# Another order of the same steps in a gated-recurrence and bilinear-FFN kernel

## The chip, the core and the metric

The kernel runs on one core of one Trainium2 chip. A core has five engines that run side by side, each from a queue of its own in the order in which the program issues: TensorE (PE in the profile, with its weight loads as PEld), VectorE (DVE), ScalarE (ACT), GpSimd (POOL) and SyncE (SP, which here only issues DMAs). The metric is device time in microseconds (us) of one execution, as the median of several runs.

## What is computed

The reference is a gated linear recurrence over time, followed by a bilinear feed-forward network on its output:

```python
for t in range(S):
    state = alpha[:, :, t, :, None] * state + np.einsum('bhd,bhe->bhde', k[:, :, t], v[:, :, t])
    y[:, :, t] = np.einsum('bhd,bhde->bhe', q[:, :, t], state)
x = y.transpose(0, 2, 1, 3).reshape(B * S, H * D)
out = (x @ w_a) * (x @ w_b) @ w_out
```

q, k, v and alpha are 4 batches x 8 heads x 768 steps x 48 in float32; w_a and w_b are 384 x 1536, w_out is 1536 x 384; the output is 3072 x 384 float32.

## The kernel before

**Chunks.** Time is cut into three stretches of 256 steps and the batches into two pairs, which makes six chunks (0 to 5). A chunk holds two batches (u = 0 and 1); each partition holds two neighbouring time steps (r), and the 128 partitions are two groups g of 64, that is, two blocks of 128 time steps. Even chunks belong to one pair of batches, odd chunks to the other, and a chunk takes over the state of the chunk two before it. Each chunk goes through a recurrence part and then a feed-forward part on its 512 tokens. PE works on the feed-forward part of one chunk while DVE, ACT and POOL prepare the recurrence of the next.

**The order** is written out by hand in a string, PROGRAM (lines 17 to 356 before). Each line names a chunk and then steps, and the kernel issues them in exactly that order: so every engine's queue is the order of its own steps in the string. A trailing letter gives the engine where there is a choice (V = DVE, S = ACT, P = POOL, Y = SP). Trailing digits on PE's steps are the PSUM banks (0 to 7) they write. A step that writes a bank or a buffer waits for its last reader.

The steps of the recurrence, with the line that does the work:

- `ld a|k|q|v` (L503) loads an input of the chunk; `W` (L483) and `Wo` (L486) load weights. SP or POOL issues them.
- `ln` (L510, ACT) takes the logarithm of alpha; `l2`, `l2s` (L518, L567) add it over the pair of time steps; `H`, `L` (L555, L561) and `R` (L577) split the sum into parts for PE; `B`, `A2`, `AQ` (L545, L592, L587) are the cumulative sums on PE.
- `E .. i|b` (L621, ACT) takes their exponentials; `ra` (L599, ACT) and `lv` (L606) adjust k and q for the second step of the pair; `mk`, `mq` (L632, DVE) scale k and q by them into QKp.
- `dk`, `de` (L654, L675) or, in later chunks, `dr`, `dl` (L638, L643: two small DMAs by way of DRAM) bring the decay of a group.
- `C`, `Ce` (L692; L914 or L916) transpose QKp on PE and copy the result out of PSUM; chunks 2 to 5 use `T` (L701, a DMA transpose issued by SP) and `Tr` (L914 or L916) in their place.
- `v`, `vs` (L725 or L727; L914 or L916) copy v into vx, straight and with the two halves of a group crossed. `vs` is two copies of 32 partitions for each u.
- `K`, `K2` (L748, L761) are the state's products, `k` (L775, or L778 and L779, DVE) updates the state; `D` (L793) are the scores; `M` (L802, DVE) masks them out of PSUM, or `Mc` (L806, ACT) copies them and `Mm` (L810, DVE) masks in SBUF.
- `SB`, `SA` (the carried state) and `Y` (inner products; all L822) add up y in PSUM, two banks for each u; `X` (L858 on ACT, L860 on DVE) copies it to xT.

The feed-forward steps: `a f w`, `b f w` (L877) are the up-projections of 128 of the 1536 columns (f = 0 to 11): three matmuls of 512 tokens (w = *), or of 256 (w = 0 or 1, one u only, which can start after that u's X). `as` (L883, ACT) copies a's bank to one of three SBUF buffers, `pr` (L891, DVE) multiplies it by b's bank. `o m h` (L899) is half of the down-projection of 128 tokens, six matmuls; `oc` (L910) the same for half the columns, at the very end; `ot`, `otc` (L914 or L916) copy the result and `st`, `stc` (L932, L935) store it.

Every matmul of the recurrence's products, scores and y is done in 64-row, 64-column pieces, four side by side; the feed-forward ones take the whole 128 x 128 array. Going from one shape to the other and back happens some 60 times in PE's order.

The loads of chunks 0 to 2, those of v for all, and all weights are on POOL's queue (chunk 0's first loads excepted); the other loads of chunks 3 to 5, the DMA transposes, the decay's DMAs and the stores are on SP's.

Of the kernel before, what the change touches and what calls it, by code (L numbers as in the profile page):

```python
# [18 lines left out]
0: B 0a 0; ld q 0b Y; E 0b i; mk 0b V; dk 0 4; E 0b b; mq 0b V; C 0 1 5; E 0a i; mk 0a V; E 0a b; fill 2 0; ld v 0 P; ld q 0a Y; mq 0a V; de 0; Ce 0 1 V; ld a 1 P  # L19
0: ln 1; cs 0 m P; C 0 0 1; Ce 0 0 V; ld k 1 P; K 0 0 2; k 0 0 V; ld q 1 P; cm 1; D 0 1 4; M 0 1; D 0 0 0; M 0 0; v 0 S; vs 0 1 V; SB 0 2; vs 0 0 V; B 1a 6  # L20
0: E 1a b; mq 1a V; E 1a i; mk 1a V; B 1b 4; W b 0 256; E 1b b; mq 1b V; dk 1 0; E 1b i; de 1; C 1 0 1; cz 0 v P; Y 0; SA 0; mk 1b V; C 1 1 0; Ce 1 0 V
0: Ce 1 1 V; D 1 0 4; ld v 1 P; K 1 0 1; K 1 1 6; X 0 S; v 1 S; Mc 1 0; D 1 1 2; Mc 1 1; W a 256 768; a 3 0 0; a 4 0 7; k 1 0 V; cz 1 q P; as 4 0; vs 1 0 V; a 5 0 1
0: W a 0 256; a 0 0 4; as 5 0; vs 1 1 V; Mm 1 0 V; SB 1 2; W b 256 768; b 4 0 5; Mm 1 1 V; cs 1 m P; b 3 0 1; a 1 0 7
1: ld a 0 P; ld a 1 P
0: k 1 1 V; a 2 0 6; as 2 0; pr 4 0; K 0 1 5; k 0 1 V; SA 1; Y 1; b 2 0 6; pr 2 0; b 1 0 5; as 1 0; pr 1 0; b 5 0 7; pr 5 0; W a 768 1536; X 1 S; c2 P
0: b 2 1 2; a 2 1 3; W b 768 1536; a 1 1 5
1: ld q 0 P
0: b 0 0 6
1: ln 0; l2 0 V; ld k 0 P
0: a 0 1 7  # L30
1: ld v 0 P
0: as 0 0; pr 0 0
1: ld q 1 P
0: as 3 0; a 5 1 0; b 0 1 4; as 2 1; pr 3 0; as 0 1; a 10 * 3; a 6 * 1
1: H 0 V; L 0 V
0: a 7 * 6; b 4 1 7; pr 2 1; a 4 1 2; pr 0 1; Wo 0 6; b 6 * 4
1: ln 1; l2 1 V; H 1 V
0: as 6 *; pr 6 *; b 10 * 1; as 10 *; a 8 * 3
1: ra 0; lv 0 q P; ld k 1 P; A2 0 4
0: as 4 1; pr 4 1; pr 10 *; a 9 * 2; a 3 1 1; Wo 6 12  # L40
1: L 1 V
2: ld a * P
1: ld v 1 P; E 0 b
0: b 8 * 7
1: E 0 i
0: as 3 1; as 9 *
2: ld q * P
1: lv 0 k V; mk 0 V
0: b 3 1 1; pr 3 1
1: dk * 4; de *  # L50
0: b 9 * 1
1: A2 1 2; mq 0 V
0: pr 9 *; as 7 *; as 8 *; as 5 1
1: E 1 b
0: b 7 * 4; pr 7 *
1: E 1 i
0: a 11 * 6; as 1 1
1: C 0 0 0; C 0 1 1
0: b 11 * 2; b 1 1 3
1: ra 1; lv 1 q P  # L60
0: pr 8 *; as 11 *; pr 11 *; b 5 1 4; pr 5 1
1: lv 1 k P
0: o 2 0 5
1: Ce 0 0 S; D 0 0 6; v 0 S; K2 0 0 0 2
0: pr 1 1; o 1 0 3; o 3 0 4
1: Mc 0 0; mq 1 V; Ce 0 1 S; D 0 1 6; k 0 0 V; SB 0 0; Mm 0 0 V; k 0 1 V; vs 0 0 S
0: o 3 1 -; ot 3 S
1: mk 1 V; C 1 0 2
2: ln *
1: vs 0 1 V; M 0 1  # L70
0: o 1 1 -
1: Ce 1 0 V
0: ot 1 S
1: v 1 V
2: l2s 0 V; l2 0 V
1: C 1 1 4; Ce 1 1 S
0: o 2 1 -
1: K2 1 1 2 3
2: ld k * P; l2s 1 V; ra 0
1: vs 1 0 S  # L80
3: ld v * P
0: cz 1 v P
1: Y 0; k 1 0 V; SA 0
0: st 3 Y
1: X 0 S; vs 1 1 V; D 1 1 6; Mc 1 1
2: R 0
1: k 1 1 V
0: o 0 0 4; o 0 1 -; c3 P
3: ld a * P
1: a 2 0 0  # L90
# [12 lines left out]
1: pr 1 0
2: AQ 6; E 1 b; E 1 i; E 0 i
1: b 10 0 1; pr 10 0; b 4 0 2; pr 4 0
2: mk 1 V; E 0 b
1: a 7 0 5; as 7 0
2: lv 1 q P
1: Y 1; SA 1; X 1 S; a 0 0 1; a 6 0 2; as 6 0
2: mq 0 V  # L110
1: b 7 0 5; pr 7 0; b 8 0 6
2: mq 1 V
1: b 5 0 7; b 6 0 2; a 3 0 3; a 10 1 4; as 5 0; pr 5 0; a 11 0 0; b 3 0 5; b 0 0 7; pr 6 0; b 10 1 2
3: ln *
2: dr
1: as 3 0; pr 3 0; a 6 1 3; as 0 0
2: T 1
1: pr 0 0; b 11 0 1; a 8 0 5
3: ra 1
1: as 11 0; pr 11 0; a 2 1 7; as 10 1; pr 10 1; b 2 1 4; a 1 1 0  # L120
2: dl
1: b 6 1 1; as 8 0; as 2 1; pr 8 0; a 0 1 2
3: l2 0 P
1: a 5 1 5; pr 2 1; a 9 0 4; b 9 0 6; b 5 1 7; as 6 1; pr 6 1
2: lv 0 k P; mk 0 V; T 0
3: v 0 S
1: as 9 0; pr 9 0; a 3 1 1; b 3 1 3; as 5 1; pr 5 1
2: K2 * * 4 5
3: vs 0 0 V; ra 0
1: b 9 1 6; as 3 1  # L130
4: ld a * Y
1: pr 3 1; a 9 1 1; o 2 0 3; o 2 1 -
2: k * 0 V; k * 1 V
3: vs 0 1 S
0: st 1 Y
1: b 0 1 7
2: Tr 1 V; v 0 S; vs 0 1 V
3: ld q * Y
1: b 7 1 4; as 0 1; pr 0 1; as 9 1; as 1 1
3: ld k * Y  # L140
1: b 8 1 2; a 7 1 5; ot 2 S
2: v 1 S; vs 1 1 P
3: l2s 0 P
1: as 7 1
4: ld k * Y
3: v 1 V
1: pr 9 1; b 1 1 3; pr 1 1; pr 7 1; a 11 1 0
2: Tr 0 S; D 1 1 6; M 1 1
1: a 4 1 1; as 4 1; a 8 1 3; o 0 0 4; as 11 1
3: l2s 1 P  # L150
1: as 8 1; pr 8 1
2: D 0 0 0; Mc 0 0; D 1 0 6; Mc 1 0
1: b 4 1 5; pr 4 1; b 11 1 2; pr 11 1
2: vs 0 0 P
1: o 0 1 -
3: R 0
0: cs 0 0 P
3: R 1
4: ln *
2: SB 0 0; SB 1 2; D 0 1 6; Mc 0 1; Mm 1 0 V  # L160
1: o 3 0 5; o 3 1 -
2: vs 1 0 S
# [12 lines left out]
4: l2s 0 V
1: o 1 0 5; o 1 1 -; ot 0 S
3: lv 0 k V
2: b 5 * 4; b 0 * 7
3: lv 1 q V; mq 1 V
2: a 7 * 0  # L180
3: E 0 i
2: as 7 *
3: lv 0 q V; mq 0 V; lv 1 k V; mk 1 V; mk 0 V
2: a 2 * 6; as 2 *
3: T 0
2: a 5 * 1; as 5 *; pr 5 *; a 3 * 0
1: ot 1 S
2: b 7 * 6; b 2 * 1; pr 2 *
3: vs 1 0 S
2: pr 7 *  # L190
3: K2 * * 2 3; k * 0 V
4: l2 0 V
2: b 4 * 4; a 4 * 1; a 0 * 5
3: k * 1 V
2: b 3 * 6; as 0 *; pr 0 *
3: T 1
4: lv 0 k V
2: as 3 *; as 4 *; pr 4 *; a 9 * 2; as 9 *; b 9 * 5
4: ra 0
2: pr 3 *  # L200
3: Tr 0 S
2: a 11 * 0; as 11 *; pr 9 *; b 11 * 1; a 1 * 2; pr 11 *; as 1 *; a 6 * 3; b 6 * 4; as 6 *; pr 6 *; b 1 * 0
5: ld a * Y
2: pr 1 *; a 8 * 1; as 8 *
3: Tr 1 V
2: b 8 * 2; a 10 * 3; as 10 *; pr 8 *
4: lv 0 q P; l2s 1 P; R 0
3: D 0 1 0; Mc 0 1; D 0 0 4; Mc 0 0; D 1 0 6; M 1 0
2: b 10 * 2; pr 10 *; o 0 0 3
3: SB 0 0  # L210
4: ra 1
3: SB 1 4; Mm 0 1 V; D 1 1 6; Mc 1 1
1: st 0 Y
5: ld q * Y; ln *
2: o 2 0 2; o 2 1 -; ot 2 S
4: R 1; lv 1 q V
5: ld k * Y
4: AQ 6
3: Mm 1 1 V; Mm 0 0 V
4: lv 1 k V; E 0 i; E 0 b  # L220
3: SA 1; vs 1 1 P
4: ld v * P
5: l2s 1 V
3: Y 0; SA 0; X 0 S; Y 1
4: mq 0 V; mk 0 V; v 1 V
2: o 1 0 2; o 1 1 -
3: X 1 S; b 2 * 6; a 11 * 0
5: l2 0 V
4: T 0
3: b 6 * 1; b 1 * 4  # L230
4: E 1 i; mk 1 V
5: ra 1
4: E 1 b
2: ot 1 S
3: a 2 * 2; as 2 *; a 6 * 5; as 6 *
5: l2s 0 V; R 0; R 1
4: dr; mq 1 V; T 1
3: a 1 * 7; as 1 *; pr 2 *; a 8 * 2
4: vs 1 0 V
2: o 0 1 -  # L240
5: ra 0
3: pr 6 *
5: AQ 6; E 1 b; E 0 i
4: K * 0 1
3: pr 1 *
5: lv 0 q V; E 0 b
3: a 3 * 4; as 3 *
5: E 1 i
4: vs 1 1 V
3: b 11 * 5  # L250
4: dl
3: b 3 * 6
5: lv 0 k V
3: pr 3 *; b 9 * 4; a 9 * 7; b 8 * 6; as 11 *; pr 11 *
2: st 2 Y
4: Tr 0 S
3: b 0 * 0
1: st 1 Y
# [798 lines left out]
```

## Time and profile before

| what | us |
|---|---|
| median of 3 runs | 193.31 (193.24 to 193.69) |
| the profiled execution | 193.74 |
| its span, first to last instruction | 191.8 |
| PE busy | 184.5 (96% of the span) |
| DVE busy | 136.8 (71%) |
| ACT busy | 114.1 (59%) |
| POOL busy | 52.9 (28%) |

The profile is one execution. A row of a timeline gives the start, the time from the first start to the last end of a group of like instructions, the engine, the line, the operation, what it writes and reads, and the count; in square brackets stands the idle time just before it and what ended that. Matmuls are pipelined: one lasts longer than the distance between two, so the time of a run of them is read from start to start. PE counts as busy while any matmul is in it, so a short wait can hide inside a busy stretch.

### The profile page before, as it was taken

The numbers are of one execution on the slowest core, as the hardware profiler recorded it, in microseconds if no ns is written. First come the engines' busy times: TensorE is split into PE (matmuls) and PEld (weight loads), VectorE is DVE, ScalarE is ACT, GpSimd is POOL, SyncE is SP. The second block draws the span as 40 slices with busy tenths as digits, with TensorE's granted clock in tenths as the row PEclk, the third lists the DMA queues.
The fourth block names the chain that finished last, engine by engine and source line by source line (L and its number), as shares of the span: only waits on it lengthen the run. The fifth ranks groups of instructions, "written<-read, shape, count | busy, mean of one in ns | idle before, by whom it ended". The sixth has DMA issues, their size and how long they took to land.

```text
span 191.8 us, 6128 instructions
## 1 busy us (share of the span) xinstructions
PE 184.5 (96%) x2597; PEld 115.2 (60%) x2613; DVE 136.8 (71%) x251; ACT 114.1 (59%) x216; POOL 52.9 (28%) x80
## 2 busy tenths in 40 slices
PE   7999999999999999999999999999999999999993
PEld 3987775666778876644446554556446555444562
DVE  2398887888998997689899996899085742234711
ACT  4446475797988888853867558775266151424321
POOL 8999506595424035000460000300030000000000
PEclk9999999999999999999999999999999999999999
DMA  5999999999994999989999988026812100210013
GB/s 137 267 221 213 254 249 239 241 265 269 252 207 86 84 205 281 257 240 156 200 296 191 180 123 201 4 82 86 177 6 82 46 3 0 82 41 3 0 68 137
DMA packets 64475, 29.41 MB, mean 153 GB/s; under 512 B 55760, under 2 KB 62816, under 8 KB 64448
## 3 DMA queue, kind: packets, MB, share of 16 engines
q1 hardware_dynamic: 46080, 16.34, 40.3%
q0 software_dynamic: 18224, 12.58, 38.0%
q8 instruction: 20, 0.33, 0.7%
q10 hardware_dynamic: 144, 0.10, 0.1%
q14 instruction: 7, 0.06, 0.1%
HBM read 25.98 MB, written 4.74 MB: 160 GB/s over the span
## 4 chain that ended last, share of the span: by engine, by line
PE 73%; DVE 12%; DMA 5%; issue 3%; ACT 3%; SPq 2%; DVEq 0%; ACTq 0%
PE psum L877 38%; PE psum L899 18%; DMA k_t<-in_k_dram 5%; PE psum L822 4%; DVE QKp L632 2%; DVE prod L891 2%; PE psum L528 2%; PE psum L692 2%; DVE vx L916 2%; PE psum L793 2%; SPq L932 1%; PE psum L748 1%; PE psum L545 1%; PE psum L910 1%; PE psum L546 1%
## 5 line engine op out<-in xcount | busy, mean ns | idle before, releaser
L877 PE MATMUL psum<-xT,wa_t 128*128 128x512 bf16 (+1 forms) x265 | 55.0, 336 | 0.6 <-DVE tmp L778 0.2
L877 PE MATMUL psum<-xT,wb_t 128*128 128x512 bf16 (+1 forms) x260 | 54.5, 335 | 0.9 <-DVE prod L891 0.3
L899 PE MATMUL psum<-wo_t,prod 128*128 128x384 bf16 x276 | 49.4, 326 | 0.0
L877 PEld LDWEIGHTS <-wa_t 128*128 128x128 bf16 x270 | 25.8, 98 | 20.6 <-issue 0.8
L877 PEld LDWEIGHTS <-wb_t 128*128 128x128 bf16 x270 | 25.5, 98 | 19.3 <-issue 0.9
L899 PEld LDWEIGHTS <-prod 128*128 128x128 bf16 x276 | 26.2, 98 | 17.6
L916 POOL COPY vx<-v_t 32x384 bf16<-32x384 bf16 x12 | 6.1, 508 | 49.8 <-ACT vx L725 40.9
L914 ACT ACTIVATE ot<-psum 128x384 f32<-128x384 f32 (+1 forms) x19 | 9.0, 472 | 11.3 <-PE psum L899 9.7
L806 ACT ACTIVATE m<-psum 128x768 bf16<-128x768 f32 x14 | 11.0, 810 | 2.9 <-PE psum L793 2.9
L606 POOL TENSOR_TENSOR q_t<-q_t,ra 128x384 f32<-128x384 f32 x4 | 4.0, 998 | 30.8 <-ACT ra L599 21.0
L916 DVE COPY ot<-psum 128x384 f32<-128x384 f32 x6 | 3.3, 557 | 11.2 <-PE psum L899 11.2
L510 ACT ACTIVATE la<-a_t 128x1536 f32<-128x1536 f32 (+2 forms) x9 | 9.5, 1054 | 2.9 <-DMA a_t<-in_alpha_dram 2.9
L858 ACT ACTIVATE xT<-psum 128x768 bf16<-128x768 f32 x10 | 7.9, 809 | 4.3 <-PE psum L822 4.3
L802 DVE TENSOR_TENSOR m<-psum,mask 128x768 bf16<-128x768 f32 x10 | 9.3, 951 | 1.3 <-PE psum L793 1.3
L632 DVE TENSOR_TENSOR QKp<-q_t,beta 128x768 bf16<-128x768 f32 x10 | 9.5, 954 | 0.6 <-DVE q_t L606 0.5
L632 DVE TENSOR_TENSOR QKp<-k_t,invb 128x768 bf16<-128x768 f32 x10 | 9.4, 953 | 0.2
L822 PE MATMUL psum<-m,vx 64*64 64x64 bf16 (+1 forms) x576 | 8.7, 205 | 0.2 <-issue 0.2
L503 POOL DMA_DIRECT2D v_t<-in_v_dram x8 | 8.5, 1063 | 0.0
L822 PEld LDWEIGHTS <-vx 64*64 64x64 bf16 x576 | 7.5, 108 | 0.6 <-issue 0.5
L725 ACT ACTIVATE vx<-v_t 128x768 bf16<-128x768 bf16 x9 | 7.6, 843 | 0.0
L822 PE MATMUL psum<-kqT,Sm 64*64 64x128 bf16 x144 | 7.6, 218 | 0.0
L914 ACT ACTIVATE vx<-v_t 32x384 bf16<-32x384 bf16 x14 | 7.3, 522 | 0.2
(278 smaller groups left out, 308.6 us busy)
## 6 DMA issues: line engine op xcount, KB each, us to landing
out_dram<-ot SPq DMA_DIRECT2D x23, 192.0 KB, 2.1
q_t<-in_q_dram SPq DMA_DIRECT2D x3, 768.0 KB, 6.2
k_t<-in_k_dram SPq DMA_DIRECT2D x3, 768.0 KB
a_t<-in_alpha_dram POOLq DMA_DIRECT2D x2, 768.0 KB, 11.3
v_t<-in_v_dram POOLq DMA_DIRECT2D x4, 384.0 KB, 11.1
a_t<-in_alpha_dram SPq DMA_DIRECT2D x2, 768.0 KB
a_t<-in_alpha_dram POOLq DMA_DIRECT2D x3, 384.0 KB, 7.8
k_t<-in_k_dram POOLq DMA_DIRECT2D x3, 384.0 KB, 6.9
```

The source lines that it names most:

```text
L503: eng.dma_start(out=t[:, us, hs].rearrange("p b h r d -> p (b h) (r d)"), in_=src[ch.b0 + us.start:ch.b0 + us.stop, hs, ch.s * 2 * C:(ch.s ...
L510: nc.scalar.activation(out=ch.la[:, us, hs].rearrange("p b h r d -> p (b h r d)"), in_=ch.a[:, us, hs].rearrange("p b h r d -> p (b h r d) ...
L632: eng.tensor_mul(QKp[ch.c % 2][:, u, j, :, hs, :D], src[:, u, hs].rearrange("p h r d -> p r h d"), f)
L725: nc.scalar.activation(out=o_, in_=i_, func=AF.Copy)
L802: nc.vector.tensor_mul(m, x, maskn())
L806: nc.scalar.activation(out=m, in_=x, func=AF.Copy)
L822: nc.tensor.matmul(o, lhsT=lhsT, rhs=rhs, start=(g, c) not in begun, stop=False, skip_group_check=True)
L858: nc.scalar.activation(out=o_, in_=i_, func=AF.Copy)
L877: nc.tensor.matmul(p, lhsT=(wa_t, wb_t)[w][:, kk, f * 128:(f + 1) * 128], rhs=ch.xT[:, kk, us, :], start=(kk == 0), stop=(kk == KT - 1))
L899: nc.tensor.matmul(op, lhsT=ch.prod[:, f, at:at + C], rhs=wo_t[:, f, :], start=(f == 0), stop=(f == NFF - 1))
L914: nc.scalar.activation(out=o_, in_=i_, func=AF.Copy)
L916: eng.tensor_copy(o_, i_)
```

## The change

The diff replaces PROGRAM and nothing else. Both strings hold the same 872 steps with the same arguments; what differs is their order, the PSUM banks, and for 60 steps the engine:

| from | to | steps |
|---|---|---|
| DVE | ACT | vs 7, ot 4, v 3, X 2, Ce 1, Tr 1 |
| DVE | POOL | lv 6, l2 3, l2s 3 |
| ACT | DVE | ot 10, Tr 3, v 3, Ce 2, X 2, vs 2, otc 1 |
| POOL | DVE | lv 2, vs 2, l2 1 |
| POOL | ACT | vs 2 |

Each queue issues its loads in the same order as before. The string is 11 lines longer or so, which shifts the line numbers of the code below it by 12. The feed-forward steps (a, b, as, pr) come in another order of f within each chunk. The head of the program, where the order of PE's recurrence steps changes most, and where the loads on POOL get other steps between them:

```diff
-0: E 1a b; mq 1a V; E 1a i; mk 1a V; B 1b 4; W b 0 256; E 1b b; mq 1b V; dk 1 0; E 1b i; de 1; C 1 0 1; cz 0 v P; Y 0; SA 0; mk 1b V; C 1 1 0; Ce 1 0 V
-0: Ce 1 1 V; D 1 0 4; ld v 1 P; K 1 0 1; K 1 1 6; X 0 S; v 1 S; Mc 1 0; D 1 1 2; Mc 1 1; W a 256 768; a 3 0 0; a 4 0 7; k 1 0 V; cz 1 q P; as 4 0; vs 1 0 V; a 5 0 1
-0: W a 0 256; a 0 0 4; as 5 0; vs 1 1 V; Mm 1 0 V; SB 1 2; W b 256 768; b 4 0 5; Mm 1 1 V; cs 1 m P; b 3 0 1; a 1 0 7
-1: ld a 0 P; ld a 1 P
-0: k 1 1 V; a 2 0 6; as 2 0; pr 4 0; K 0 1 5; k 0 1 V; SA 1; Y 1; b 2 0 6; pr 2 0; b 1 0 5; as 1 0; pr 1 0; b 5 0 7; pr 5 0; W a 768 1536; X 1 S; c2 P
-0: b 2 1 2; a 2 1 3; W b 768 1536; a 1 1 5
...
-1: ln 0; l2 0 V; ld k 0 P
+0: E 1a b; W a 768 1536; c2 P; vs 0 0 V; B 1b 4; W b 768 1536; dk 1 6; E 1b i; M 0 1
+1: ld q 0 P
+0: Y 0
+1: ld k 0 P
+0: mk 1a V; SA 0; E 1b b; mq 1a V; mk 1b V; C 1 0 7; K 1 1 2; mq 1b V; Ce 1 0 V; C 1 1 3; v 1 S; Ce 1 1 V; de 1; K 1 0 4; k 1 0 V; k 1 1 V; D 1 0 6; X 0 S
+0: a 2 0 0; a 4 0 1; Mc 1 0; vs 1 1 V; as 4 0; vs 1 0 V; a 5 0 3; D 1 1 4; Mc 1 1; SB 1 6; Mm 1 1 V; a 1 0 1; Mm 1 0 V; b 4 0 2; as 1 0; pr 4 0; a 3 0 4; as 3 0
+0: b 0 0 1; K 0 1 5; SA 1; Y 1; a 0 0 2; as 2 0; b 2 0 0; k 0 1 V; X 1 S; b 3 0 4; pr 3 0
+1: ln 0; l2 0 P
...
+1: l2 1 P
...
+1: ld q 1 P
+0: Wo 0 6; a 1 1 5; a 0 1 0; as 0 1
+1: ra 0; lv 0 q P
+0: b 0 1 2; pr 0 1; a 10 * 3; a 7 * 0; as 4 1; b 4 1 1
...
+0: b 1 1 6; b 5 1 7; b 7 * 4
+1: L 1 V
+0: pr 7 *
+1: A2 0 0; E 0 i; E 0 b; mq 0 V
```

In chunk 0 `Ce 0 1` and `vs 0 1` also go from DVE to ACT. The steps around the crossing from chunk 2 to chunk 3 (SP's queue had `2 T 1; 2 dl; 2 T 0; 4 ld a; 0 st 1; 3 ld q; 3 ld k` and now has `0 st 1; 2 T 1; 2 dl; 2 T 0; 4 ld a; 3 ld q; 3 ld k`):

```diff
-2: Mm 0 0 V; Mm 0 1 V; Y 1; X 1 V
...
-2: Y 0; X 0 S
...
-3: lv 0 k V
...
-3: lv 1 q V; mq 1 V
...
-3: lv 0 q V; mq 0 V; lv 1 k V; mk 1 V; mk 0 V
...
-3: K2 * * 2 3; k * 0 V
+3: lv 0 k V; dr
+4: ld q * Y
+3: lv 0 q P; mq 0 V
+2: a 9 * 0; as 1 *
+3: mk 0 V
+2: a 11 * 1; as 11 *; a 8 * 7
+3: lv 1 q V; lv 1 k V; mk 1 V; mq 1 V
+2: b 9 * 2; b 11 * 1; b 8 * 3; pr 11 *
...
+3: K2 * * 1 7
```

Before it stand, after the change, `3 E ..` on ACT, `1 ot 0 V; 2 Y 1; Mm 0 1 V; SA 1; X 1 S; Mm 0 0 V; Y 0`, and `2 X 0 V`. In chunk 4 the order is now `D 1 0 6; Mc 1 0; .. K * 0 2; k * 0 V; M 0 1`, then `3 b 10 * 6; b 4 * 7; pr 4 *; b 5 * 2; pr 5 *`, then `4 SB 1 0; SB 0 4`, then `3 a 7 * 3; a 10 * 7; o 3 0 2`. The end of the program still is the last `oc`, its copy on ACT and its store on SP.

## The prediction

> **What bounds the kernel now.** I read the page's head and its chain first, then busy time by stretch, then TensorE's own order of work.
>
> ```profile
> span 191.8 us, 6128 instructions
> ...
> PE 73%; DVE 12%; DMA 5%; issue 3%; ACT 3%; SPq 2%; DVEq 0%; ACTq 0%
> ```
>
> ```profile
> 96.00:114.00 18.00, 17.45 (x294) 9.84 (x298) 17.52 (x28) 11.71 (x20) 2.99 (x4) 1.00 1.34 206
> ```
>
> TensorE (PE) holds 73% of the chain. In the second view the columns are span, then PE, PEld, DVE, ACT and POOL busy: between 96 and 114 us VectorE (DVE) is as full as PE, so DVE decides there whether PE waits. PE's timeline shows how tight its order is, and where it is not:
>
> ```profile
> 14.82 0.91 PE L654 MATMUL psum<-og,la 128*48 128x2 f32 x32
> ...
> 21.39 0.49 PE L877 MATMUL psum<-xT,wa_t 128*128 128x256 bf16 x3
> 22.06 0.49 PE L877 MATMUL psum<-xT,wa_t 128*128 128x256 bf16 x3 [0.17 <-DVE tmp L778]
> 22.80 0.49 PE L748 MATMUL psum<-v_t,QKp 64*64 64x48 bf16 x16 [0.26 <-DVE prod L891]
> ...
> 23.92 1.48 PE L877 MATMUL psum<-xT,wb_t 128*128 128x256 bf16 x12
> 25.24 0.82 PE L877 MATMUL psum<-xT,wa_t 128*128 128x256 bf16 x6
> ...
> 27.21 2.11 PE L877 MATMUL psum<-xT,wa_t 128*128 128x512 bf16 x8
> 29.15 0.49 PE L877 MATMUL psum<-xT,wb_t 128*128 128x256 bf16 x3
> ...
> 29.80 0.38 PE L877 MATMUL psum<-xT,wb_t 128*128 128x512 bf16 x1
> ```
>
> Twelve 256-column matmuls take 25.24 - 23.92 = 1.32 us from start to start, so a **half step** (three of them) costs 0.33. The three 512-column steps between 27.21 and 29.15 (one of nine records is missing) give 0.65 for a **full step**. Such steps run back to back almost everywhere. The steps at 21.39 and 22.06 instead last 0.67 and 0.74: each hides 0.33 us of waiting for a PSUM bank that DVE still reads. Comparing every step with the usual length of its kind, PE waits 2.3 us in all between 9 and 24 us, and 2.3 us after that. Two of the later waits:
>
> ```profile
> 52.33 1.45 PE L877 MATMUL psum<-xT,wa_t 128*128 128x256 bf16 x9
> 53.62 0.49 PE L877 MATMUL psum<-xT,wb_t 128*128 128x256 bf16 x3
> ...
> 87.28 0.70 PE L761 MATMUL psum<-v_t,QKp 64*64 64x48 bf16 x64 [0.42 <-DVE QKp L632]
> ```
>
> The first hides 0.3 (53.62 - 52.33 = 1.29 for three half steps of 0.98), the second some 0.5; two more near 99 and 104.5 have 0.35 and 0.4, the rest less than 0.1 each. The end:
>
> ```profile
> 188.71 0.33 ACT L914 ACTIVATE ot<-psum 128x192 f32<-128x192 f32 x1 [0.66 <-PE psum L910]
> ```
>
> So the kernel is a start of 9 us, PE's fixed work with 4.6 us of waits, and a tail of 3.3 us after the last matmul (about 188.5 to 191.8).
>
> **The change part by part.** The multiset of steps is the same, so PE's work is the same. I count 60 changes between 128- and 64-row matmul shapes before and 59 after: 0.1 us at most. What can change the time is the waits.
>
> *Engines.* Sixty steps change engine: from DVE 18 go to ScalarE (ACT) and 12 to GpSimd (POOL); 23 come from ACT to DVE and 5 from POOL; 2 go from POOL to ACT.
>
> ```profile
> L606 POOL TENSOR_TENSOR q_t<-q_t,ra 128x384 f32<-128x384 f32 x4 | 4.0, 998 | 30.8 <-ACT ra L599 21.0 <-DMA q_t<-in_q_dram 7.7 <-PE psum L587 2.1
> ...
> L606 DVE TENSOR_TENSOR q_t<-q_t,ra 128x384 f32<-128x384 f32 x6 | 3.3, 546 | 0.0
> ```
>
> At the mean of each kind (these two rows price the largest exchange, 1.00 us on POOL for 0.55 on DVE) DVE loses about 1.3 us over the whole program and ACT gains about 1.0. POOL does nine more two-input operations (21 for 12), 9.0 us, and eight copies fewer. The sums by themselves move nothing: what counts is what stands where. The loads leave each queue in the same order.
>
> *The head.* Up to chunk 0's second decay product (the row at 14.82) PE's order is the same, and I change nothing before 15.7 (14.82 + 0.91). Now Y 0 and SA 0 stand there directly, ahead of C 1 0, so the first y is complete at 16.5. ACT must first finish two more operations that were behind or elsewhere (v 1, de 1), so its X 0 runs about 16.85 to 17.65.
>
> ```profile
> 17.36 0.81 ACT L858 ACTIVATE xT<-psum 128x768 bf16<-128x768 f32 x1 [1.23 <-PE psum L822]
> 18.97 1.71 DVE L916 COPY vx<-v_t 32x384 bf16<-32x384 bf16 x4
> 112.77 0.51 DVE L916 COPY vx<-v_t 32x384 bf16<-32x384 bf16 x2
> ```
>
> Before it ended at 18.17, so the first up-projection starts near 18.35 instead of 19.0. Then DVE's four vx copies: 1.71 us before, beside POOL's load issues, against 0.51 for two where POOL is idle. After the change POOL has stopped issuing at that point (its next step waits for ACT's second ln), so they should take 1.0. With that the waits at 22.06 and 22.80 go: bank by bank, I find the previous reader done before PE arrives, with only 0.1 us lost at b 0. Y 1 then ends near 22.3 instead of 23.9, with seven half steps done instead of eight: 1.6 - 0.3 = **1.3 us ahead**.
>
> What is late next are the weights.
>
> ```profile
> 15.58 0.76 POOL L483 DMA_DIRECT2D wa_t<-in_moe_w_a_dram  x1
> ...
> 16.87 0.79 POOL L483 DMA_DIRECT2D wb_t<-in_moe_w_b_dram  x1
> ```
>
> ```profile
> wa_t<-in_moe_w_a_dram POOLq DMA_DIRECT2D x1, 576.0 KB, 10.4
> wb_t<-in_moe_w_b_dram POOLq DMA_DIRECT2D x1, 576.0 KB, 11.9
> ```
>
> The last thirds of both land at 15.58 + 10.4 = 26.0 and 16.87 + 11.9 = 28.8, and POOL's queue up to them is unchanged. PE now wants them at 25.6 and 28.6, so it waits 0.4 and 0.2. At 28.85 it has done 21 half and 2 full steps; before, it had done 20 and 3 at 29.80. That is 0.95 us earlier with 0.32 us less done: **0.6 us of the lead is left**. The pair-sums and the loads behind them on POOL are issued up to 8 us later, which I cost at nothing: q, k, v and w_out lie behind a queue that is still delivering w_b at 28.8; if that cover were gone, w_out's first half, issued near 28, would land near 40 by w_b's 11.9 us, 0.3 late for its first use at 39.7.
>
> *The middle.* I gave each PE step after 28.85 the usual length of its kind and compared the time at which it is due with the queue of the engine that feeds it, and with the last reader of its bank. All waits of before would go: PE ends at 185.4 instead of 188.5, **3.1 us** less (0.6 + 2.3 + 0.1 and rounding). The margins that I find are mostly 0.4 to 0.8 us; the smallest: Mm 0 0 of chunk 2 done 76.95 for Y 0 at 77.5; pr 11 of chunk 2 done 84.85 for chunk 3's K2 at 85.4; M 0 1 of chunk 4 done 122.9 for SB 1 at 123.5; pr 4 and pr 5 of chunk 3 at 124.1 and 124.8 for steps at 124.6 and 125.2. The wait at 87.28 has its cause on SP's queue:
>
> ```profile
> 67.48 2.20 SPq L932
> ...
> 70.27 10.47 DMA k_t<-in_k_dram
> 80.83 0.56 DVE k_t L606
> ```
>
> Chunk 3's k is issued behind a store and two transposes, lands at 80.7, and DVE's whole chain to K2 starts with it. The store now stands ahead of the transpose, and the transposes' inputs come about 1.5 us sooner, so k should land near 77, before DVE is free for it at 79.1.
>
> *The tail* is the same chain (last oc, its copy on ACT, its store); I cost it at nothing.
>
> *What I take.* Bounds from the rows: at best no new wait, -3.1 us; at the other end each margin of some 0.5 us is overrun several times, as DVE's full stretch shows it can be. DVE's copies, loads' landings and POOL's holds are what I can place only to some tenths. I take half of the old middle waits as coming back in new places, 1.2 us: 3.1 - 1.2 = **-1.9 us**. The profiled execution took 193.74, 1.94 outside its span, and the median of the runs is 193.31, 0.43 below it. So 193.74 - 1.9 = 191.8 for an execution like the profiled one, and 193.3 - 1.9 = 191.4 for the median.
>
> **Rivals.**
>
> *No new wait.* The margins hold: -3.1, 190.2. For it: they hold on paper everywhere. Against: before, PE waits 2.3 us in the middle, for landings and held operations that a count of durations doesn't show.
>
> *The gain is given back at chunk crossings.* New waits of 2.5 to 3.7 us, for instance chunk 3's k and q landing no sooner because SP's ring is full (the 2.20 us of one store issue at 67.48): 192.7 to 193.9. For it: between the landing and K2 stand seven DVE operations in a row, about 5 us. Against: 1.5 us of margin there by my count.
>
> *Slower: POOL holds DVE.*
>
> ```profile
> 50.49 0.99 POOL L606 TENSOR_TENSOR k_t<-k_t,a_t 128x384 f32<-128x384 f32 x1 [4.71 <-DVE lh L577]
> 50.67 1.02 DVE L779 TENSOR_TENSOR S<-tmp,bl 128x192 bf16<-128x192 f32 x1
> 22.04 0.36 DVE L779 TENSOR_TENSOR S<-tmp,bl 128x192 bf16<-128x192 f32 x1
> ```
>
> The same multiply of two SBUF tiles takes 0.36 us alone and 1.02 beside POOL's two-input operation, ending 0.2 us after it. It is the source of the wait at 52.33. A hit costs 1.02 - 0.36 = 0.66 us of DVE. The order before has one such hit; most of its POOL operations stand beside DVE work that reads PSUM, which is not lengthened. With nine more of them, nine more hits cost 5.9 us, and where DVE is full PE pays them: 193.3 - 3.1 + 5.9 = 196.1. From five hits on (3.3 us) the change is no gain. The likeliest place is chunk 3's lv 0 q, which POOL may start near 77.1 while DVE's Mm 0 0 is due to end at 76.95. Against it: by my times 18 or more of the 21 fall beside PSUM work or where DVE waits for them anyway. The Trainium skill, GPSIMD Engine Reference, section Specifications, states this sharing: contention with VectorE instructions in a two-port mode or with two SBUF inputs. By that rule the result is this rival's; the trace agrees where the two met, at 50.67 (1.02 us).
>
> *The change doesn't do what it says*: the copies stay beside POOL's issues. Then 0.7 us of the head's lead goes, and as the weights cap that lead anyway, the time is the forecast's within 0.2 us. It needs no case of its own.
>
> **How the numbers follow.** Chances: the forecast with new waits of 0.5 to 2.5 us (190.8 to 192.7) 0.47; no new wait 0.18; given back 0.14; slower 0.21. A measurement of this kernel tells 0.3%, 0.6 us, from no change. So faster by more than that 0.47 + 0.18 = 0.65, within it 0.14, slower 0.21. The range of 190.0 to 194.2 takes in the floor and the given-back case and leaves out most of the slower one.
>
> **What would show it.** Right: xT's first copy on ACT near 17.7, Y 1 ending near 22.3, then PE waiting for DMA at the first step of a 10 and of b 7, and A2 of chunk 1 near 29.5 (31.6 before); k_t of chunk 3 landing by 79; no DVE row of two SBUF inputs over 1 us. Wrong: gaps in PE's 512-column steps beyond 1.5 us after 30 us, their releaser DVE behind POOL, or a DMA. What would make the prediction wrong most easily is a single late tile in the full stretch of DVE, 79 to 127 us, since everything behind it on DVE's queue moves with it.

## The result, and the profile after

| what | before | after |
|---|---|---|
| median, us | 193.61 (8 runs, 192.32 to 194.38) | 191.73 (8 runs, 191.31 to 192.61) |
| ratio | | 0.992, 95% interval 0.9897 to 0.9943 |
| the profiled execution, its span | 193.74, 191.8 | 191.33, 189.5 |
| start of PE's last step | 188.01 | 185.83 |

The change is faster: by the ratio 1.5 us (1.1 to 2.0), by the medians 1.9. A later set of 12 runs of the same kernel (c1 below) gave 0.9968 (0.9942 to 0.9995), 0.6 us (0.1 to 1.1). The two intervals only just meet, so the gain is taken here as some 0.6 to 1.5 us, and the profiled execution after is one of the shortest.

The head of the page and its chain, then busy time between 96 and 114 us (span, then PE, PEld, DVE, ACT, POOL):

```profile
span 189.5 us, 6112 instructions
...
PE 88%; DMA 4%; DVE 3%; issue 2%; POOL 2%; ACT 1%; POOLq 0%; ACTq 0%
```

```profile
96.00:114.00 18.00, 17.87 (x295) 10.07 (x295) 16.58 (x25) 13.67 (x23) 2.60 (x3) 1.00 1.06 173
```

PE's share of the chain went from 73% to 88%, DVE's from 12% to 3%. In that stretch DVE came down from 17.52 to 16.58 of 18 us and ACT up from 11.71 to 13.67: DVE is no longer full where it had set the pace. PE's own order of work in the head and at the places where it waited before:

```profile
14.42 0.91 PE L666 MATMUL psum<-og,la 128*48 128x2 f32 x32
...
19.64 0.50 PE L889 MATMUL psum<-xT,wa_t 128*128 128x256 bf16 x3
20.57 0.50 PE L889 MATMUL psum<-xT,wb_t 128*128 128x256 bf16 x3 [0.43 <-DVE vx L928]
...
23.09 0.50 PE L889 MATMUL psum<-xT,wa_t 128*128 128x256 bf16 x3
...
26.38 1.46 PE L889 MATMUL psum<-xT,wa_t 128*128 128x512 bf16 x5
27.67 2.12 PE L889 MATMUL psum<-xT,wb_t 128*128 128x256 bf16 x15
29.44 0.53 PE L604 MATMUL psum<-lh,utr 128*128 128x384 f32 x1
```

```profile
52.48 0.49 PE L889 MATMUL psum<-xT,wb_t 128*128 128x256 bf16 x3
52.81 0.49 PE L889 MATMUL psum<-xT,wa_t 128*128 128x256 bf16 x3
```

```profile
83.83 1.89 PE L889 MATMUL psum<-xT,wb_t 128*128 128x512 bf16 x8
85.65 0.70 PE L773 MATMUL psum<-v_t,QKp 64*64 64x48 bf16 x64
```

The steps near 52 us are 0.33 apart again (0.3 was lost there), and chunk 3's K2 stands directly behind its forerunner without the 0.42 in brackets that the row at 87.28 had. In the head the wait moved: 19.64 to 20.57 is 0.93 for a half step that takes 0.33, so 0.6 is lost ahead of the first b.

**Where the 2.18 us of the profiled pair came from** (188.01 to 185.83). 0.40 was there before the orders part: the second decay product starts at 14.42 in place of 14.82. From there to the end of Y 1 (23.92 to 23.09) it is 0.43 more, but with seven half steps done in place of eight (0.33): a real 0.1. The other 1.68 lies behind Y 1, 1.5 of it in waits of more or less size that the table below counts from 57.5 us or that stood at 52 us. So in this pair the head gave almost nothing and the middle gave nearly all. The first 0.40 isn't the change: c1, the changed kernel once more, has 14.95 at this place, and the mean of four profiles with the old order up to there (before, e2, f2, i1) is 14.60, that of eight with the new (after, c1, e1, e4, f1, g1, g3, h1) 14.58. What sets it in one run isn't shown. One thing does vary at the start: both programs start alike, and yet PE's weight loads at line 546 (558 after) have two speeds, whose change comes at different times. Weight loads before, then after, x2 each:

```profile
5.25 0.66 PEld L545 LDWEIGHTS psum<-la,ut 128*128 128x128 f32 x2
5.88 0.66 PEld L546 LDWEIGHTS psum<-la,ut 128*128 128x128 f32 x2
```

```profile
5.21 0.60 PEld L557 LDWEIGHTS psum<-la,ut 128*128 128x128 f32 x2
5.78 0.35 PEld L558 LDWEIGHTS psum<-la,ut 128*128 128x128 f32 x2
```

In 14 profiles of this case the second cumulative sum of chunk 0 starts anywhere from 5.51 to 6.84, 6.27 and 6.69 for one and the same program. The Trainium skill, TensorE: Matmul & The Clock Gate, section What's actually happening, says why such a start varies: the window after which the clock rises is free-running and doesn't begin with the kernel. The runs agree that it varies; what it costs they show too: little, since the start of the second decay product (14.27 to 14.75 in ten of the profiles, 14.82 to 16.04 in the other four) doesn't follow it: it is 14.46 behind 5.51 in f1, 14.27 behind 5.86 in g1 and 14.64 behind 6.69 in h1.

### The profile page after: what moved, and what is told of

It reads as the page before. It is cut to its first block, busy times and chain, and to the rows that moved or that the text cites. A ratio compares the mean times of both kernels' runs of the same rounds, so it can differ in the third digit from the quotient of the medians.

```text
span 189.5 us, 6112 instructions
## 1 busy us (share of the span) xinstructions
PE 183.1 (97%) x2597; PEld 114.6 (60%) x2613; DVE 135.3 (71%) x246; ACT 117.2 (62%) x220; POOL 57.7 (30%) x81
## 3 DMA queue, kind: packets, MB, share of 16 engines
HBM read 25.98 MB, written 4.74 MB: 162 GB/s over the span
## 4 chain that ended last, share of the span: by engine, by line
PE 88%; DMA 4%; DVE 3%; issue 2%; POOL 2%; ACT 1%; POOLq 0%; ACTq 0%
PE psum L889 47%; PE psum L911 24%; PE psum L834 6%; DMA a_t<-in_alpha_dram 4%; PE psum L805 2%; PE psum L704 2%; PE psum L599 1%; DVE prod L903 1%; PE psum L922 1%; PE psum L773 1%; PE psum L760 1%; PE psum L666 1%; PE psum L557 1%; PE psum L558 1%; DVE vx L928 1%
## 5 line engine op out<-in xcount | busy, mean ns | idle before, releaser
L926 ACT ACTIVATE ot<-psum 128x384 f32<-128x384 f32 (+1 forms) x12 | 5.7, 478 | 17.9 <-PE psum L911 15.3
L618 POOL TENSOR_TENSOR q_t<-q_t,ra 128x384 f32<-128x384 f32 x7 | 7.0, 1007 | 28.0 <-ACT ra L611 26.9
L926 ACT ACTIVATE vx<-v_t 32x384 bf16<-32x384 bf16 x28 | 14.6, 521 | 0.5
L579 POOL TENSOR_TENSOR l<-la 64x384 f32<-64x384 f32 x6 | 6.0, 994 | 26.0 <-PE psum L889 11.3
L928 DVE COPY ot<-psum 128x384 f32<-128x384 f32 (+1 forms) x13 | 7.0, 536 | 7.5 <-PE psum L911 7.0
L822 DVE TENSOR_TENSOR m<-m,mask 128x768 bf16<-128x768 bf16 x14 | 7.4, 551 | 0.4 <-ACT m L818 0.3
```

What stands on the lines that cost most here:

```text
L926: nc.scalar.activation(out=o_, in_=i_, func=AF.Copy)
L928: eng.tensor_copy(o_, i_)
```

## The experiments

Two theories went into the runs. **Head**: the prediction's, by which the reordered start is worth 0.6 us. **Middle**: formed from the two traces, by which the head is even and the gain is PE's waits after it. For every kernel I took each PE step's start-to-start time less the usual one of its kind, as the prediction did, and summed it from 57.5 us to the end:

| order in the middle | kernels | PE waits after 57.5 us |
|---|---|---|
| old | before, e1, f1 | 2.03, 1.85, 1.82 |
| new | after, c1, e4, f2, g3 | 0.83, 0.94, 0.82, 0.95, 0.83 |
| new | g1, e2, h1 | 1.12, 1.33, 1.47 |
| new, POOL's steps back | g2 | 2.47 |
| new, all engines back | e3 | 7.52 |
| old, POOL's steps new | i1 | 11.51 |

i1's figure isn't waits alone: some 4 us of it are matmuls at half the clock (see i1). A second count needs no usual lengths: from the start of A2 of chunk 1 to the start of PE's last matmul, less 1.63 us for the five half steps that the new order still has to do there. It is 156.8 and 156.4 in the old order (before, e1), 155.2, 155.2, 155.2, 155.8, 155.9 and 156.0 in the new (after, e4, g3, c1, h1, g1), and 156.7 in the new order with POOL's steps back (g2). By the means the new middle is 1.0 us shorter.

The diffs below are cut to the steps that carry the experiment, within lines too; steps that only changed their line in the string are left out.

**e1, new head, old rest.**

```diff
+0: as 3 0; b 0 0 1; K 0 1 5; SA 1; Y 1; a 0 0 2; as 2 0; b 2 0 0; k 0 1 V; X 1 S; as 5 0; b 3 0 1; pr 2 0; b 1 0 5; pr 1 0; b 5 0 7; pr 5 0; b 2 1 2; a 2 1 3
+0: a 1 1 5
+1: ln 0; l2 0 V
```

> The new order up to X 1 of chunk 0, then the old order of all steps that are left. Middle theory (read from the two traces: the head is even, PE's waits after 24 us fell from 2.35 to 0.7 us): no gain, 0 to 0.3 us less than before, ratio 0.998 to 1.0, and the old waits come back: 0.3 us at a 5 0 of chunk 1, 0.5 ahead of chunk 3's K2, 0.35 and 0.4 near chunk 3's last score and SA 0. Head theory (the prediction's share): 0.6 us less or more, ratio 0.997 or lower, with those waits shorter because DVE starts earlier.

Measured 0.9994 (0.9971 to 1.0017): the Middle theory's. Of the four old waits that it named, two came back (0.33 at chunk 3's last score, 0.29 at its SA 0); a 5 0 of chunk 1 had none, and chunk 3's K2 0.14 where before had 0.49. At the joint two banks and two a buffers are written by later steps before their reader (f = 0, 1 and 3 of chunk 0 are other values; the work is the same).

**e2, old head, new rest.**

```diff
 0: SA 1; Y 1; b 2 0 6; pr 2 0; b 1 0 5; as 1 0; pr 1 0; b 5 0 7; pr 5 0; W a 768 1536; X 1 S
+0: c2 P; W b 768 1536
+1: ld q 0 P; ld k 0 P
+0: as 3 0; b 0 0 1; pr 3 0
+1: ln 0; l2 0 P
+0: a 4 1 6
+1: ln 1; ld v 0 P; H 0 V
+0: as 0 0; pr 0 0
```

> The old order up to X 1 of chunk 0, then the new order of all steps that are left. Middle theory: nearly the whole gain, 1.4 to 1.8 us less than before, ratio 0.991 to 0.993, less than 0.9 us of PE waits after 24 us. Head theory: 1.0 to 1.3 us less, ratio 0.993 to 0.995.

Measured 1.005 (1.0025 to 1.0076), by neither. The joint makes a wait of its own: a 2 1 takes the bank of a 0 0, which `as 0 0` reads, and ACT reaches that only after both `ln`.

```profile
24.52 0.49 PE L889 MATMUL psum<-xT,wa_t 128*128 128x256 bf16 x3
26.45 0.81 PE L889 MATMUL psum<-xT,wa_t 128*128 128x256 bf16 x6 [1.45 <-ACT as__625 L895]
```

That is 1.6 us (1.93 less 0.33), 0.8% of the time. Without it e2 would stand near 0.997, which is still above both ranges, so e2 supports neither theory. (Here f = 0 and 3 of chunk 0's first half share a bank, so one product has other values.)

**f1 and f2, the joint at 50 us**, where both orders have done the same steps but three.

```diff
 1: X 0 S; a 4 0 0; vs 1 1 S; k 1 0 V
+2: ra 0
+1: k 1 1 V; a 2 0 2
+2: R 1
+0: ot 0 S; ot 2 S; st 0 Y
```

> The new order up to k 1 0 of chunk 1 (about 50 us, where both orders have done the same steps but three), then the old order; two steps at the joint moved to fit the banks. Middle theory (PE's waits of the two traces, 2.2 us before 50 us in both, 2.4 against 0.5 after it): 0 to 0.5 us less than before, ratio 0.9975 to 1.0, and the old waits stand again: ahead of chunk 3's K2, near chunk 3's last score and at its SA 0, about 1.7 us in all. Head theory (the prediction's 0.6 us of lead lasts): 0.6 us or more less, ratio under 0.997.

```diff
 1: X 0 S; vs 1 1 V; D 1 1 6; Mc 1 1
 2: R 0
 1: k 1 1 V
+0: o 0 0 4; o 0 1 -; c3 P
+3: ld a * P
+1: a 4 0 0
```

> The old order up to the same place, then the new one; ot 2 of chunk 0 moved ahead of chunk 2's AQ to fit the banks. Middle theory: 1.2 to 1.7 us less than before, ratio 0.991 to 0.994, under 0.7 us of PE waits after 50 us. Head theory: 0.5 to 1.0 us less, ratio 0.995 to 0.9975.

f1 measured 1.0106 (1.0075 to 1.0137), f2 1.0023 (1.0006 to 1.0039). Neither is in its range. f2's profile explains itself: `ot 2`, moved ahead of AQ, made AQ wait on DVE.

```profile
51.56 0.34 PE L599 MATMUL psum<-l,utb 64*64 64x384 bf16 x2
53.26 0.36 PE L599 MATMUL psum<-l,utb 64*64 64x384 bf16 x2 [1.36 <-DVE ot L928]
```

Between the same steps 1.7 us are lost, 0.9%; without them f2 would stand near 0.9935, inside the Middle range (a subtraction, not a measurement), and its waits after 57.5 us are the new order's (0.95). f1 has the old order's (1.82), a joint wait of 0.6 at chunk 1's D 1 0 and 0.85 at b 7 in the head, and its PE ends 0.2 later than before's. That is not the 2 us of the ratio: the profiled run is the shortest of its six (194.07, median 195.13), and where the others lose 1 us more stays open.

**e3, the new order on the old engines.**

```diff
-1: l2 0 P
+1: l2 0 V
...
-2: X 0 V
+2: X 0 S
```

> The new order and banks, but each of the 60 steps on its old engine (POOL back from 21 two-input operations to 12). If POOL beside DVE costs DVE time (the prediction's slower rival): as fast as the changed kernel or faster, ratio 0.990 or lower. If the order decides and the engines are only fitted to it: between, 0.5 to 1.2 us slower than the changed kernel, ratio 0.994 to 0.998, waits for DVE in the stretch 79 to 127 us. If order and engines only work together: no gain or slower than before, ratio 1.0 or more.

Measured 1.0527 (1.0488 to 1.0565), 10 us: the third case. Its waits, by what ended them (us in total, times, longest):

```profile
PE psum L834 <- DVE m L822: 2.2, 2, 1.4
...
PE psum L911 <- DVE kqT L928: 1.1, 1, 1.1
PE psum L834 <- DVE Sm L787: 1.1, 1, 1.1
```

The prediction counted the 60 moves as 1.3 us off DVE and 1.0 onto ACT. Undone in the new order they cost 10 us against before and 11 against the changed kernel (203.09, 192.14). The sums of the lengths don't give that; PE pays for the place of a step.

**i1, the old order with POOL's new steps.**

```diff
-1: ln 0; l2 0 V; ld k 0 P
+1: ln 0; l2 0 P; ld k 0 P
```

> The order before the change with only the engines of the 15 pair-sums and level steps as after it (12 from DVE to POOL, 3 from POOL to DVE). If POOL's help alone carries the gain: 1 to 2 us faster than before, ratio 0.990 to 0.995. If it needs the order that was made around it: no gain or slower, ratio 1.0 to 1.02, with PE waiting for level steps that POOL does in 1.0 us and, at the start, for loads that wait behind pair-sums on POOL's queue.

Measured 1.0961 (1.0921 to 1.1001). The second case, and five times the 2% that I allowed it. POOL, DVE and PE of i1, in that order:

```profile
32.33 0.93 POOL L515 DMA_DIRECT2D k_t<-in_k_dram  x1
...
37.27 1.04 POOL L618 TENSOR_TENSOR k_t<-k_t,a_t 128x384 f32<-128x384 f32 x1
38.34 0.96 DVE L644 TENSOR_TENSOR QKp<-k_t,invb 128x768 bf16<-128x768 f32 x1 [4.78 <-POOL k_t L618]
...
39.70 1.38 PE L889 MATMUL psum<-xT,wb_t 128*128 128x512 bf16 x3 [3.98 <-DVE prod L903]
```

lv 0 k takes 1.04 us on POOL, but it stands behind five load issues (32.33 to 37.27). DVE's mk waits 4.78 us for it, the products queued behind mk wait too, and PE waits 3.98 for a bank. Here one such step costs four times its own length. The new order issues these loads at other places.

Not all of i1's loss of some 19 us is waits. In three stretches, in or within 2 us of its three longest PE waits (3.98 to 39.70, 3.26 to 57.61, 2.55 to 130.16), PE's granted clock was half: 0.50 in 39.8 to 43.2, 56.9 to 63.6 and 132.0 to 135.3. The page's row of the clock, in 40 slices, and twelve like matmuls before and in the second stretch:

```profile
PEclk9999999789959999999999999699999999999999
```

```profile
47.48 2.12 PE L911 MATMUL psum<-wo_t,prod 128*128 128x384 bf16 x12
...
59.36 4.02 PE L911 MATMUL psum<-wo_t,prod 128*128 128x384 bf16 x12
```

By the start-to-start times this adds some 5.7 us. So i1 prices the old order with POOL's steps, but not a late step alone.

**g2, the new order with only POOL's 15 steps back.**

```diff
-3: lv 0 q P; mq 0 V
+3: lv 0 q V; mq 0 V
```

> The changed kernel with the 15 pair-sums and level steps (l2, l2s, lv) back on their old engines: 12 from POOL to DVE, 3 from DVE to POOL; POOL again does 12 two-input operations. If POOL's operations beside DVE cost DVE more than they take off it (the prediction's slower rival): faster than the changed kernel, ratio under 0.990. If POOL takes them off DVE where DVE is the fuller: 12 x 0.55 - 3 x 0.55 = 5 us more on DVE, of which PE pays 0.5 to 3 us in the stretches 79 to 127 us, ratio 0.995 to 1.008.

Measured 1.002 (1.0 to 1.004): 1.0% above the changed kernel's first ratio, 0.5% above its control's. Its waits after 57.5 us are 2.47 against 0.83 to 0.95, among them 0.28 ahead of chunk 3's K2, where the changed kernel has none, and this:

```profile
104.80 0.34 PE L599 MATMUL psum<-ll,utb 64*64 64x384 bf16 x4
105.67 0.69 PE L834 MATMUL psum<-m,vx 64*64 64x128 bf16 x45 [0.54 <-DVE m L822]
```

So POOL takes off DVE what PE waited for: the 15 changes of engine together are worth 1.0 us of time (193.48 against 192.47 in g1 beside it) and 1.0 to 1.65 us of these waits. Which of the 15 do it, one run can't tell. The K2's wait isn't lv 0 q's alone: e2, where POOL does that step, has 0.31 there, and the old order 0.49, 0.14 and 0.07 (before, e1, f1).

**g3, two more steps of chunk 3 on POOL.**

```diff
-3: lv 1 q V; lv 1 k V; mk 1 V; mq 1 V
+3: lv 1 q P; lv 1 k P; mk 1 V; mq 1 V
```

> The changed kernel with two more steps of chunk 3, lv 1 q and lv 1 k, on POOL in place of DVE: three two-input operations of 1.0 us in a row from about 77.5, the last of them beside DVE's own work on two SBUF tiles (lv 0 k, mq 0, mk 0). If POOL holds DVE (the slower rival's mechanism): the DVE operations that it meets take up to 0.7 us longer each (lv 0 k near 1.0 in place of 0.55, mq 0 or mk 0 near 1.4 to 1.9 in place of 0.95), DVE saves 1.1 and pays 0.5 to 1.2. If not: 0.55 and 0.95 as they are, and DVE's chain to chunk 3's K2 ends 1.1 us earlier. In both cases K2 has some 0.3 us of margin, so the time changes by less than 0.3 us unless the chain gets longer by more than that.

Measured 0.9931 (0.9909 to 0.9954) beside the control's 0.9968 (0.9942 to 0.9995): not told apart. The mechanism is there, though. POOL and DVE of g3:

```profile
80.40 1.37 POOL L618 TENSOR_TENSOR k_t<-k_t,a_t 128x384 f32<-128x384 f32 x1
```

```profile
80.36 0.56 DVE L618 TENSOR_TENSOR k_t<-k_t,a_t 128x384 f32<-128x384 f32 x1
80.84 1.75 DVE L644 TENSOR_TENSOR QKp<-q_t,beta 128x768 bf16<-128x768 f32 x1
```

mq 0 takes 1.75 for 0.95, and POOL's step 1.37 for 1.0. The rows fit taking turns: lv 0 k on DVE began 0.04 us ahead of POOL's step and took its usual 0.56; POOL's step, begun at 80.40, was 0.37 late and ended at 81.77; mq 0, begun at 80.84, ended 0.82 behind that. DVE saved 1.1 us and paid 0.8: its last scaling ends 1.30 us ahead of chunk 3's K2 (85.20, 86.50), in the changed kernel 0.94 (84.71, 85.65), and K2 had no use for the difference.

**g1, the store behind the transposes again.**

```diff
-0: st 1 Y
...
 2: T 1
...
 4: ld a * Y
+0: st 1 Y
```

> The changed kernel with one step of SP's queue put back: the store of chunk 0's second output block stands behind chunk 2's transposes, the decay load and chunk 4's alpha, as before the change. By the prediction's reading chunk 3's k then lands at about 80.8 again in place of before 79.5, DVE's chain to chunk 3's K2 starts 1.3 us later, the K2 at 85.65 waits 0.3 to 0.6 us, and the kernel loses that: 0.2 to 0.5 us slower than the changed kernel, ratio 0.993 to 0.995. Rival: the k load's landing is set by the DMA queues' own pace and not by its issue, so it lands within 0.5 us of 79.5, no wait, ratio as the changed kernel's.

Measured 0.9977 (0.9953 to 1.0002). SP and DVE of the changed kernel, then of g1, where PE is 2.25 us later at that point:

```profile
68.82 7.51 SPq L515 DMA_DIRECT2D k_t<-in_k_dram  x2
...
79.55 0.56 DVE L618 TENSOR_TENSOR k_t<-k_t,a_t 128x384 f32<-128x384 f32 x1
```

```profile
71.52 7.38 SPq L515 DMA_DIRECT2D k_t<-in_k_dram  x2
...
82.22 0.56 DVE L618 TENSOR_TENSOR k_t<-k_t,a_t 128x384 f32<-128x384 f32 x1 [0.33 <-DMA k_t<-in_k_dram]
```

DVE does wait 0.33 for k, but K2 (88.08) doesn't: the order of SP's queue is worth a third of a microsecond of DVE, and nothing of PE. What g1 lost came earlier, in its first 35 us, by the causes that follow.

**c1, the changed kernel again; e4 and h1, its first b step moved.**

> The changed kernel itself once more, as the measure for the other three of this call, and for how much its start varies. Landing theory (from eight profiles: the second third of w_b landed anywhere between 20.2 and 22.1 us, the last between 28.8 and 30.1, at like issue times): its b 4 0 of chunk 0 waits 0.4 to 1.7 us for the second third, its first b 7 starts within 0.3 us of the last third's landing or waits for it, and the ratio to before lies between 0.990 and 0.997. DVE theory (the release that the first profile names at b 4 0): the wait there is 0.6 again whatever the landing.

```diff
-0: a 1 0 1; Mm 1 0 V; b 4 0 2; as 1 0; pr 4 0; a 3 0 4; as 3 0
-0: b 0 0 1; K 0 1 5
+0: a 1 0 1; Mm 1 0 V; as 1 0; a 3 0 4; as 3 0
+0: b 0 0 2; b 4 0 1; pr 4 0; K 0 1 5
```

> The changed kernel with one PE step moved: b 4 0 of chunk 0 stands behind a 3 0 and b 0 0 (and its product with it; two banks exchanged), so it comes some 0.7 us after it is asked for now. Cause A, the second third of w_b, which lands at 20.52: the 0.6 us wait after a 1 0 goes, Y 1 ends near 22.5 in place of 23.1, and then PE waits for the last thirds at a 10 (landing 26.0) and b 7 (28.8), 0.2 us each, so A2 of chunk 1 starts 0.2 to 0.3 us earlier than 29.44 and the kernel gains 0.2 us, ratio 0.991. Cause B, DVE (the release that the profile names): b 4 0's place changes nothing, a wait of about 0.6 stays at whatever stands there.

```diff
-0: a 2 0 0; a 4 0 1; Mc 1 0
+0: a 2 0 0; a 5 0 3; Mc 1 0
...
-0: a 5 0 3; D 1 1 4
+0: a 1 0 1; as 1 0; D 1 1 4
...
-0: a 1 0 1; Mm 1 0 V; b 4 0 2
+0: a 4 0 1; Mm 1 0 V; b 1 0 2
```

> The changed kernel with f = 1 and f = 4 exchanged in chunk 0's first half: a 5, a 1, then a 4, b 1 where a 4, a 5, a 1, b 4 stood, so the first up-projection by w_b takes columns of its first third (landed by 14.5 in most runs) and b 4 0 comes some 3.5 us later. Landing theory: no wait at that b step, Y 1 of chunk 0 starts 0.4 to 1.5 us earlier than in the control of this call (bound next by DVE's mask, near 21.7), and then PE waits at a 10 and b 7 for the last thirds, so that A2 of chunk 1 comes at the last landing plus 0.5 to 0.7 us: 0 to 0.8 us gained on the control. DVE theory: the wait stays at that place and nothing is gained.

c1 measured 0.9968 (0.9942 to 0.9995), e4 0.9956 (0.9935 to 0.9977), h1 0.995 (0.9928 to 0.9973): no difference that these tell. The profiles tell more. c1's wait, and e4's:

```profile
20.66 0.50 PE L889 MATMUL psum<-xT,wa_t 128*128 128x256 bf16 x3
21.84 0.50 PE L889 MATMUL psum<-xT,wb_t 128*128 128x256 bf16 x3 [0.68 <-DMA wb_t<-in_moe_w_b_dram]
```

```profile
21.11 0.49 PE L889 MATMUL psum<-xT,wb_t 128*128 128x256 bf16 x3
22.06 0.50 PE L889 MATMUL psum<-xT,wb_t 128*128 128x256 bf16 x3 [0.46 <-DMA wb_t<-in_moe_w_b_dram]
```

b 4 needs w_b's second third, which landed at 20.52 in the first profile, 21.79 in c1 and 22.01 in e4; PE starts 0.05 us behind it each time. The name DVE in the first profile's bracket was a neighbour: vx ended at 20.53 (19.40 + 1.13), a hundredth after the landing. In h1 the wait is gone (0.2 us is left at a 4, b 1 and a 3 together), and SA 1 starts at 22.24 against 23.29. But A2 of chunk 1 starts at 30.43 against 30.45: everything was given back between. In e4 and f1 it was given back to the last thirds, as the prediction had it (0.28 at a 10 and 0.28 at b 7 in e4, 0.2 and 0.85 in f1). f1's b 7:

```profile
29.49 0.82 PE L889 MATMUL psum<-xT,wb_t 128*128 128x512 bf16 x3 [0.68 <-DMA wb_t<-in_moe_w_b_dram]
```

In h1 the last third had landed at 28.65; there it was another thing. POOL, DVE and PE of h1, in order of time:

```profile
25.75 0.92 POOL L515 DMA_DIRECT2D v_t<-in_v_dram  x1
25.84 2.08 DVE L567 CAST lh<-l 128x384 fp32r<-128x384 f32 x1 [0.41 <-POOL l L530]
...
26.68 1.01 POOL L530 TENSOR_TENSOR l<-la 128x384 f32<-128x384 f32 x1
...
28.33 0.49 PE L889 MATMUL psum<-xT,wb_t 128*128 128x256 bf16 x3 [0.53 <-DVE prod L903]
```

The changed kernel's profile, the same two steps:

```profile
25.79 0.93 POOL L515 DMA_DIRECT2D v_t<-in_v_dram  x1
```

```profile
25.88 0.36 DVE L567 CAST lh<-l 128x384 fp32r<-128x384 f32 x1 [0.41 <-POOL l L530]
```

H 0 of chunk 1 is a cast of 0.36 us. It is released by POOL's pair-sum, as is POOL's next step, the issue of a load: both start within 0.1 us of each other every time. In six of the eight profiles with this order it took 0.36; in two (h1, g1) 2.07, until 0.2 us after POOL's next two steps were over. Then the products behind it on DVE are 1.7 us late, and PE waits 0.7 + 0.33 in h1 and 0.45 + 0.33 in g1. g1 loses 0.7 more at 35.87, behind A2, to another hold: mq 0 of chunk 1, 0.95 in the changed kernel's first profile, took 2.46. POOL and DVE of g1:

```profile
32.38 0.94 POOL L515 DMA_DIRECT2D k_t<-in_k_dram  x1
33.33 1.02 POOL L618 TENSOR_TENSOR k_t<-k_t,a_t 128x384 f32<-128x384 f32 x1
```

```profile
32.71 2.46 DVE L644 TENSOR_TENSOR QKp<-q_t,beta 128x768 bf16<-128x768 f32 x1 [0.50 <-POOL q_t L618]
```

## Why the prediction was right, and where it wasn't

The sign, the size (191.4 forecast, 191.73 measured) and the range held. In the later set (c1, 192.14) the gain was a third of the 1.9 us forecast, so the close hit of the first set is partly luck. Of the sum's two terms one failed and one held.

**The head** (0.6 us of lead) is the term that failed. Its first steps came as forecast: xT's first copy ended at 17.57 (17.65), the last thirds landed at 25.98 and 28.80 (26.0, 28.8), A2 started at 29.44 (29.5). But Y 1 ended at 23.09, not 22.3, and A2's time came out right by two errors that cancelled. I had compared every step with PSUM's banks and only the last thirds' landings; the first b asks for the second third, and waits 0.4 to 1.7 us for it in every profile of the new head on its own engines but h1's. Then PE comes too late to wait for the last thirds. And 29.44 was a good run: with the order unchanged to there, f1, g3, c1 and g1 had 29.96, 30.29, 30.45 and 31.02. The new order has five half steps fewer done at that point (1.63 us at 0.325); with them the five stand at 31.1 to 32.7, 31.9 in the mean, against 31.6 and 31.4 for the old head (before, f2). So by these profiles (five against two) the head is no gain but a loss of some 0.35 us in the mean, from 0.45 gained to 1.1 lost. The later loads, which I cost at nothing, did cost nothing: w_out's first half, issued at 28.60, landed at 37.55.

**The middle** (2.3 us of waits gone, 1.2 coming back) was right in size and place: from 57.5 us on 1.9 in the mean of the old order's three kernels, 0.9 in the mean of the new one's first five and 1.04 in that of all eight, so 0.9 to 1.0 less, and 1.0 less by the second count; forecast was 2.3 - 1.2 = 1.1. PE's last step came 0.92 behind my no-wait sum (185.83 against 188.01 - 3.1 = 184.91) in many pieces of 0.02 to 0.15. The margins that I listed as the smallest held. Head and middle together, +0.35 - 1.0 = -0.65, is close to c1's 0.6. The first eight runs, at -1.5, would need better heads than the mean; the one of them that was profiled has one, the other seven left no profile.

**Causes inside the middle.** I gave the K2's wait to SP's order; g1 shows that it gives DVE 0.33 us and PE none. With POOL's steps back (g2) 0.28 of it returns, but as it is 0.07 to 0.49 in the old order and 0.31 in e2, what sets it in one run stays open. The likeliest trouble that I named for that step, holding DVE's Mm 0 0, didn't come: POOL did it from 77.53 to 78.54, after the mask.

**The slower rival** was right as a mechanism and wrong as a sum. Held operations are there: ll at 27.15 takes 1.03 for 0.56 in the changed kernel's first profile, the cast 2.07 in two of eight, mq 0 of chunk 3 1.75 in g3, and mq 0 of chunk 1 1.79, 1.80 and 2.46 in h1, e2 and g1. But POOL's steps as a whole save PE 1.0 to 1.65 us of waits (g2). And its longest hold over the usual length wasn't the one that I had looked at, two SBUF inputs beside arithmetic, but a cast of one input that starts together with a load's issue.

**Copies beside POOL's issues**: forecast 1.0 us for the four in place of 1.71; they took 1.13. I had said that POOL has stopped issuing there; it issued until 19.67, 0.27 into them.

```profile
19.40 1.13 DVE L928 COPY vx<-v_t 32x384 bf16<-32x384 bf16 x4
```

```profile
18.75 0.92 POOL L515 DMA_DIRECT2D k_t<-in_k_dram  x1
```

## What to carry to other kernels

When a reordered start comes earlier, look up the landing of everything that its steps read, piece by piece: the load that is late next need not be the last one. A step moved to another engine costs what stands ahead of it on that queue, which here was four times its own length. Compare starts over several profiles before believing a few tenths: a start that leans on landings gives another answer in each run.

## What the runs showed of the hardware that was not expected

- A cast from SBUF to SBUF was held by POOL for two of its steps on end (0.92 + 1.01, cast 2.08 in place of 0.36) or not at all, with the same 0.07 to 0.09 us between POOL's start and its own. The Trainium skill, SBUF — State Buffer, section Who interferes with whom, says that casts can enter a mode that contends with GpSimd, and that whoever issues first gets the shared pair for the whole instruction while the other fully blocks. The block agrees. That six of eight casts weren't held behind a load issue that had begun first, and two were held through a second instruction, is more than the section says; what decides it stays open. To issue that load ahead of the pair-sum, where POOL is idle for 5 us, might keep the two apart; it wasn't tried.
- In g3 DVE and POOL were both longer than alone (DVE 1.75 for 0.95, POOL 1.37 for 1.0), and yet the rows fit one at a time, each held by the one that began before it.
- In i1 the granted clock was half (0.50) for 3.4, 6.8 and 3.4 us, in or within 2 us of PE waits of 3.98, 3.26 and 2.55 us: twelve of 384 columns took 3.82 us from start to start in place of 2.05. The longest idle time of PE in the other kernels, 1.51 us (g1), was followed by none.
- Loads with nearly the same issue time land far apart: w_b's second third, issued from 12.62 to 13.24, landed from 20.2 to 22.1 us, the last third, issued from 16.6 to 17.1, from 28.65 to 30.1.
